# Free choice of PSUM banks, a new order table, and 114 VectorE instructions handed to GpSimd

## The chip, the cores and the metric

The kernel runs on one core of a Trainium2 chip. A core has five engines that work side by side and meet only at semaphores: TensorE (PE, the matmuls), ScalarE (ACT, the exponentials), VectorE (DVE), GpSimd (POOL) and SyncE (SP, which issues the DMAs). Operands lie in SBUF; matmul results land in PSUM, which has eight banks of 512 fp32 values for each of the 128 partitions. The metric is the device time of one execution in microseconds (us).

## The reference

Input x has 2048 rows of 640 values, in bfloat16. The output is `x + s * g`, with

```python
xn = _layernorm(x, axis=-1)
s = _A_ref(xn, A_wqkv, A_wo)                       # attention, 32 heads of 20
g = _silu(_B_ref(xn, B_w1, B_w2, B_w3, B_w4))
# A: qkv = xn @ wqkv; p = softmax(q k^T * 20**-0.5); s = (p v) @ wo
# B: h = gelu(layernorm(xn) @ w1); hs = [four quarters of h, shifted by 1, -1, 2, -2 rows] @ w2
#    x1 = xn + hs; result = x1 + gelu(layernorm(x1) @ w3) @ w4
```

So there are three layer norms: the one of x, the one inside `B` before w1, and the third one, of x1, before w3. The bulk of the work is the softmax: 32 heads times 2048 x 2048 exponentials.

## The kernel before

**Tasks and the order table.** The Python code does not issue instructions in the order in which it is written. Each piece of work is a task (`T(engine, cost, function, reads, writes, ...)`): a group of matmuls, one ACT, DVE or GpSimd instruction, or a DMA issue. After all 5483 tasks are known, `Planner.follow(TABLE)` reads a long string, `TABLE`: two characters name the next task, and one more character per acquisition says which banks (or which buffers) it takes. The string thus fixes the order of the instructions on every engine and the place of every PSUM tile. Each engine then works through its own list in that order, and a semaphore wait stands wherever a task needs another engine's result or a bank that another task has to give back. The costs, the `due` times and constants such as `c_pool`, `dma_bw` and `dma_lat0` only feed the planner that wrote the table; they issue nothing.

**Attention.** The heads are worked in eight quads of four heads, each quad in four groups of 512 queries (`attn_quad`): 32 groups. A group goes over 16 key tiles of 128 keys. For each key tile, PE makes scores (keys on the partitions, 512 queries, four heads: four banks), something turns scores into exp(scores), and PE multiplies these with the values into one bank, bank 7, which gathers the whole group (L1233 and L1367). A score tile (two heads, 1024 columns, two neighbouring banks) goes one of two ways:

- ACT takes the exponential straight out of PSUM (L1432, 788 instructions of 1024 columns; L1414 does two tiles in one instruction).
- Up to eight key tiles of a group are *block units*: two key tiles in a block, mostly two blocks in a unit. In a unit, ACT does half of each key tile. DVE does the other half with integer arithmetic: an eviction (L1459, tasks `u...`) writes 16-bit integers whose bit pattern is approximately exp as a bfloat16, and three more *bit pieces* per unit (L1358, tasks `s<quad>_<group>_<block>_<v>`, v = 1, 2, 3) add a constant to all 4096 integers (2048 in a unit of one block). Each of the four variants (the eviction's own and three pieces) is then multiplied with the values (L1367, tasks `pvd...`), and the four together average the error out.

**Two ways to make a score tile.** In row mode (L1375, `score`) the matmul takes the 32 partitions of one head, and the four heads use the four row groups of the array. In column mode (L1390) the queries lie in a zero-padded copy, and a tile takes eight matmuls of 128 rows and 32 columns. A task marked `flex` (496 single ACT tiles, `score_act`) takes row mode where the task before or behind it on PE is also in row mode, and column mode elsewhere; so the table decides that too.

**PSUM.** Banks 0 to 6 are handed out by `pl.kind(...)` in `build`: `S` (a score tile) may lie in banks 0-1 or 2-3; `W` (any projection or MLP tile, `mm_tile`, L640) in bank 4, 5 or 6; `SD` (the two score tiles of one block key: one for ACT, one for DVE) in one of the two pairs plus two of banks 4 to 6, or in both pairs. The transposes at the start use banks 0 to 3 in turn, and a task `gate` stands between them and the first score.

**End of a group.** `normalise`: DVE transposes bank 7 into SBUF (L1480), takes the reciprocal of the sums (L1482), multiplies (L1488, tasks `onT`, the reciprocal product), transposes back (L1490, tasks `on`), and SP stores the result to DRAM.

**Around it.** Everything else (projections of later heads, the whole of B, the output projection) is cut into `W` tiles that the table strews between the scores: PE makes a tile (L640), DVE evicts it (L1109, L1171, L1712, L1744, L1783, L1798, L1567 ...). The third norm is L872 on DVE, 16 of its 25 instructions, each 640 values out of and into SBUF. At the end, `finish_qc` adds x to each of 16 row tiles (L1628, tasks `cmb0` to `cmb15`, both inputs in SBUF) and stores them. The last group is worked in two halves (`last_half`) so that its output projection can begin early. GpSimd has memsets, small powers (L862), four early norms (L868, L910) and 17 scalings of values (L1179, L1512).

Of the kernel before, what the change touches and what calls it, by code (L numbers as in the profile page):

```python
# [57 lines left out]
class Planner:  # L58
    def __init__(self):
# [14 lines left out]
        self.dma_bw = 223.0  # L74
        self.dma_lat0 = 1900.0
# [141 lines left out]
    def follow(self, table):  # L217
# [24 lines left out]
        while at < len(table):  # L242
# [7 lines left out]
            st = max(row_at + 6.0, row_end[t.part]) if e == "pe" and pe_mode and t.mode else eng_free[e]  # L250
# [27 lines left out]
            if e == "pe":  # L278
                if t.mode != pe_mode:
                    t.finish += self.mode_cost  # L280
                if t.mode:
                    row_at = t.finish - t.dur
                    row_end[t.part] = t.finish
                pe_mode = t.mode
# [169 lines left out]
class Cfg:  # L454
# [5 lines left out]
    def __init__(self, S=2048, D=640, H=32, F=1536):  # L460
# [26 lines left out]
        self.AHEAD = 2  # L487
        self.UNITS = ((),
# [3 lines left out]
                      ((0, 0, 2), (1, 1, 2), (3, 0, 2), (5, 1, 2)))  # L492
# [25 lines left out]
            [4, 3, 2, 4])  # L518

# [44 lines left out]
def c_pe(ninstr, N):  # L564
    return ninstr * max(14.0, 0.106 * N)
# [5 lines left out]
def c_pool(n, kind="ts"):  # L571
    return 150 + (1.1 if kind == "ts" else 2.4) * n


class Gen:
# [8 lines left out]
    def alloc(self, name, shape, dtype):  # L584
# [4 lines left out]
        off = self.pl.alloc(name, n * esz)  # L589
# [26 lines left out]
    def T(self, eng, dur, fn, reads=(), writes=(), name="", **kw):  # L616
        kw.setdefault("cls", self.cur_cls)
        return self.pl.task(eng, dur, fn, reads=reads, writes=writes, name=name, **kw)
# [28 lines left out]
    def build(self, plan_only=False):  # L647
        nc, pl = self.nc, self.pl
        with contextlib.ExitStack() as es:
            ARENA = 212480  # L650
# [7 lines left out]
            pairs = [(0, [0, 1]), (0, [2, 3])]  # L658
            high = [(0, [4, 5]), (0, [5, 6]), (1, [4, 6])]
            third = [(1, x[1]) for x in high[:2]]  # L660
            pl.kind("W", "B", [(0, [4]), (0, [6]), (1, [5])])
            pl.kind("S", "B", pairs + (third if self.cfg.THIRD else []))
            pl.kind("SD", "B", [(r + q, x + y) for r, x in pairs for q, y in high]
                    + ([(3, pairs[0][1] + pairs[1][1]), (3, pairs[1][1] + pairs[0][1])] if self.cfg.FALL else []))
            pl.kind("SR", "B", [(r + q, x + y) for r, x in pairs for q, y in high[:2]]
                    + [(3, pairs[0][1] + pairs[1][1]), (3, pairs[1][1] + pairs[0][1])])
            pl.kind("SW", "B", [(0, [2, 3, 4, 5])])
            pl.hold = {"pe": self.cfg.HPE, "dve": self.cfg.HDVE}
            if self.cfg.SAVE:
                pl.saves = {"SD": "W", "SR": "W", "SW": "W"} if self.cfg.SAVE != 3 else {"SD": "W"}  # L670
                pl.reserve = self.cfg.RESERVE
                pl.hard = self.cfg.SAVE == 2
            pl.pool("PT", 7)
            pl.kind("PT", "PT", [(0 if i == 6 else 1, [i]) for i in range(7)])
            pl.kind("PT2", "PT", [(0, [i, i + 1]) for i in (0, 2, 4)])
# [13 lines left out]
    def program(self):  # L689
# [14 lines left out]
        self.T("pe", 0, None, writes=[("S", b) for b in range(4)] + [("gate",)], name="gate")  # L704
# [62 lines left out]
    def alloc_persistent(self):  # L767
# [37 lines left out]
        for b in range(4):  # L805
            self.pl.pe_psum_atoms.add(("S", b))
        self.pl.pe_psum_atoms.update([("PV", 0), ("wob",), ("ktp",), ("gate",)])
# [27 lines left out]
    def ln_tiles(self, tag, tiles, dst_of, dst_atoms_of, ve_out=None):  # L835
# [28 lines left out]
        for li, n in enumerate(tiles):  # L864
# [6 lines left out]
            T("dve", c_dve(D, "4x") + 140,  # L871
# [67 lines left out]
    def ln1_and_transpose(self):  # L939
# [13 lines left out]
        for g in range(4):  # L953
            for kc in range(cfg.KC):
                b = bk % 4
                act = bk in cfg.TRA
                bk += 1
                for bi in range(4):
                    n = 4 * g + bi
                    def fn(e, n=n, bi=bi, b=b, kc=kc):  # L960
                        pb = self.bank(b, BF16)
# [5 lines left out]
                    T("pe", c_pe(4, 128), fn, reads=[A("xn", n), A("ident")], writes=[("S", b)], name=f"tr_x{g}_{kc}_{n}")  # L967
                d = xnT[:, kc, 512 * g:512 * g + 512]
                if act:
                    T("act", c_act(512), lambda e, d=d, b=b: e.activation(d, self.bank(b, BF16)[:, 0:512], AF.Copy),  # L970
                      reads=[("S", b)], writes=[A("xnT", kc, g)], name=f"trev_x{g}_{kc}")
                else:
                    T("dve", c_dve(512, "2x"), lambda e, d=d, b=b: e.tensor_copy(d, self.bank(b, BF16)[:, 0:512]),
                      reads=[("S", b)], writes=[A("xnT", kc, g)], name=f"trev_x{g}_{kc}")
# [366 lines left out]
    def block_bits(self, quad, qc, blocks, ends):  # L1341
# [9 lines left out]
        for v in range(4):  # L1351
            if v == 0:
                dst, dsta = U[:, ub, 0:w], halves
            else:
# [3 lines left out]
                T("dve", c_dve(w, "4x"), lambda e, v=v, dst=dst: e.tensor_scalar(dst, U[:, ub, 0:w], EXP_B[v], None, op0=ALU.add),  # L1358
# [19 lines left out]
    def score_act(self, b, qc, kt, a, gb=None):  # L1378
# [4 lines left out]
        def fn(e):  # L1383
            for jj in range(2):
# [4 lines left out]
                for c in range(4):  # L1389
# [4 lines left out]
                    reads=[("gate",), A("KT", b, kt // 4), A("QT", b, qc), A("QTa", b, qc)] + ([] if gb is None else [A("QM", gb)]),  # L1394
# [3 lines left out]
    def score_rows(self, b, qc, kt, wide):  # L1398
# [7 lines left out]
        T("pe", 207, fn, reads=[("gate",), A("KT", b, kt // 4), A("QT", b, qc), A("QTa", b, qc)],  # L1406
# [31 lines left out]
    def score_both(self, b, qc, kt, a, quad, r):  # L1438
# [14 lines left out]
        T("pe", 207, fn, reads=[("gate",), A("KT", b, kt // 4), A("QT", b, qc), A("QTa", b, qc)], writes=[sa, da],  # L1453
# [12 lines left out]
    def normalise(self, quad, qc):  # L1466
# [22 lines left out]
        T("dve", c_dve(512, "1x"), fnn, reads=[A("Ob"), A("RZ", ob)], writes=[ota], name=f"onT{quad}_{qc}", cls=cls)  # L1489
# [115 lines left out]
    def finish_qc(self, qc):  # L1605
# [8 lines left out]
        for nl in range(4):  # L1614
# [13 lines left out]
            T("dve", c_dve(cfg.D, "2x"), lambda e, sl=sl, addend=addend, res=res: e.tensor_tensor(res, SB2[:, sl, :], addend, op=ALU.add),  # L1628
# [131 lines left out]
    def b_w34(self, c0):  # L1760
# [29 lines left out]
        for hh in range(2):  # L1790
# [3 lines left out]
            for n in range(4 * c0, 4 * c0 + 8):  # L1794
# [10 lines left out]
                T("dve", c_dve(2 * D, "1x"),  # L1805
# [7 lines left out]
    r"###^#6#q#_#f#(#3$)#]#}#)#$#7#[$9#8$D$Z#c$O&p#9#`#:#a#;#d#%#<#0#b&q#=&o$#$*#>#e#~#?(m#&#,$$#@(n#/$+#'#A#*$%#-#B$&$,#C#+#2$'#D#1#.#s$($-#E#F#u#G#H#v#I#4"  # L1813
# [119 lines left out]
```

## Time and profile before

| what | value |
|---|---|
| time, median of 3 runs (lowest to highest) | 863.0 us (862.06 to 863.29) |
| span of the profiled execution, first to last instruction | 859.6 us |
| busy: ACT / PE / DVE / POOL | 815.5 / 800.6 / 734.7 / 39.3 us |
| ACT exponentials of 1024 columns | 788 x 1039 ns |
| DVE evictions of a unit, 1024 columns | 189 x 1213 ns |
| DVE bit pieces of 4096 / 2048 | 150 x 1216 ns / 24 x 680 ns |
| mean granted TensorE clock | 0.988 of full speed |

The profiled execution is one by itself; the profile gives its span, and no other time of its own is shown. The median of the timed runs is 3.4 us above that span, which is taken as what lies before the first and behind the last instruction. An engine's busy time is the union of its instructions. A line such as "L1432 ACT ACTIVATE arena<-psum 128x1024 bf16<-128x1024 f32 x788" names the source line, the engine, the operation, output and input with their shapes, and the number of instructions. The name `arena` is the one SBUF tensor that holds everything. In the views of waits, the engine that stood still is on the left, and what released it is behind the arrow. Durations of neighbouring instructions of one engine overlap a little, since one begins while the one before it still drains.

### The profile page before, as it was taken

How to read it: one execution, taken by the hardware profiler on the slowest of the kernel's cores; microseconds unless marked ns; L12 is line 12 of the kernel's file. 1: busy time of each engine (PE TensorE's matmuls, PEld its weight loads, DVE VectorE, ACT ScalarE, POOL GpSimd, SP SyncE). 2: the span in 40 equal slices, each digit the busy share in tenths (PEclk: the TensorE clock that was granted, in tenths of full speed). 3: DMA queues.
4: the chain of work that ended last, by engine and by line, in shares of the span. 5: the costliest groups of instructions: out<-in, count | busy, mean ns of one | idle time of the engine just before them, and what ended most of it. 6: DMA issues, size and time to landing. Idle time of an engine off the chain costs nothing.

```text
span 859.6 us, 31925 instructions
## 1 busy us (share of the span) xinstructions
PE 800.6 (93%) x14542; PEld 338.8 (39%) x14542; DVE 734.7 (85%) x1031; ACT 815.5 (95%) x854; POOL 39.3 (5%) x75
## 2 busy tenths in 40 slices
PE   7999999999899999999988999999997899989996
PEld 4443333334344433333433444343333343424464
DVE  7649999998998899999877999998995889987655
ACT  7799999999999999999999999999999999999994
POOL 5510000000000000000000000000000000000000
PEclk9999999999999999999999999999999999999998
DMA  7000533222110022311033011313211102041312
GB/s 230 18 16 24 137 97 89 90 66 65 25 40 16 18 50 55 79 44 46 11 94 92 14 51 27 81 36 89 50 32 47 34 13 54 13 123 33 116 57 95
DMA packets 74487, 50.83 MB, mean 59 GB/s; under 512 B 44768, under 2 KB 69552, under 8 KB 74352
## 3 DMA queue, kind: packets, MB, share of 16 engines
q1 hardware_dynamic: 74352, 48.79, 21.1%
q8 instruction: 115, 1.88, 0.9%
q14 instruction: 20, 0.16, 0.1%
HBM read 34.53 MB, written 10.17 MB: 52 GB/s over the span
## 4 chain that ended last, share of the span: by engine, by line
ACT 63%; PE 29%; DVE 7%; issue 1%; DMA 1%; SPq 0%; DVEq 0%
ACT arena L1432 57%; PE psum L640 10%; PE psum L1375 5%; PE psum L1390 4%; PE psum L1367 3%; PE psum L1233 3%; DVE arena L1459 2%; ACT arena L1787 2%; PE psum L1274 1%; ACT arena L1803 1%; DVE arena L1358 1%; ACT arena L1414 1%; ACT arena L1716 1%; DVE arena L852 1%; PE psum L963 1%
## 5 line engine op out<-in xcount | busy, mean ns | idle before, releaser
L1432 ACT ACTIVATE arena<-psum 128x1024 bf16<-128x1024 f32 x788 | 733.1, 1039 | 20.8 <-PE psum L1375 17.8
L640 PE MATMUL psum<-arena 128*32 128x320 bf16 (+1 forms) x5952 | 359.2, 335 | 0.6 <-DVE arena L1459 0.2
L1459 DVE TENSOR_SCALAR arena<-psum 128x1024 uint16<-128x1024 f32 (+1 forms) x243 | 263.7, 1094 | 31.8 <-PE psum L1375 30.5
L640 PEld LDWEIGHTS psum<-arena 128*32 128x32 bf16 x5952 | 148.8, 97 | 132.6 <-issue 31.2
L1375 PE MATMUL psum<-arena 32*128 32x512 bf16 x1384 | 165.6, 387 | 34.6 <-ACT arena L1432 24.2
L1358 DVE TENSOR_SCALAR arena<-arena 128x4096 uint16<-128x4096 uint16 (+1 forms) x174 | 194.7, 1142 | 2.9 <-PE psum L1367 1.8
L1390 PE MATMUL psum<-arena 128*32 128x512 bf16 x2400 | 182.7, 381 | 3.1 <-ACT arena L1432 2.1
L1233 PE MATMUL psum<-arena 128*22 128x512 bf16 x1552 | 148.9, 383 | 2.4 <-ACT arena L1432 2.0
L1367 PE MATMUL psum<-arena 128*22 128x512 bf16 x1728 | 146.2, 381 | 3.3 <-DVE arena L1358 3.1
L1375 PEld LDWEIGHTS psum<-arena 32*128 32x128 bf16 x1384 | 42.0, 91 | 179.5 <-ACT arena L1432 115.1
L1390 PEld LDWEIGHTS psum<-arena 128*32 128x32 bf16 x2400 | 46.1, 95 | 69.3 <-ACT arena L1432 57.7
L1367 PEld LDWEIGHTS psum<-arena 128*22 128x22 bf16 x1728 | 40.6, 91 | 53.6 <-issue 15.5
L1233 PEld LDWEIGHTS psum<-arena 128*22 128x22 bf16 x1552 | 38.8, 91 | 49.9 <-issue 18.6
L1109 DVE CAST arena<-psum 128x512 bf16<-128x512 f32 x40 | 27.0, 682 | 11.7 <-PE psum L640 11.4
L1783 DVE CAST arena<-psum 128x512 bf16<-128x512 f32 x48 | 32.7, 681 | 3.0 <-PE psum L640 2.5
L1567 DVE SCALAR_TENSOR_TENSOR arena<-psum,arena 128x320 bf16<-128x320 f32 x32 | 15.5, 489 | 22.5 <-PE psum L640 22.3
L1171 DVE CAST arena<-psum 128x320 bf16<-128x320 f32 x32 | 15.1, 486 | 16.2 <-PE psum L640 16.0
L852 DVE BATCH_NORM_STATS2 arena<-arena 128x6 f32<-128x320 bf16 x54 | 23.7, 477 | 3.2 <-DMA arena<-in_A_x_dram 3.1
L1480 DVE STREAM_TRANSPOSE arena<-psum 128x512 f32<-128x512 f32 x31 | 21.9, 708 | 1.7 <-PE psum L1367 1.2
L1490 DVE STREAM_TRANSPOSE arena<-arena 128x512 bf16<-128x512 bf16 x31 | 21.8, 702 | 0.2
L1744 DVE TENSOR_TENSOR arena<-psum,arena 128x320 bf16<-128x320 f32 x32 | 15.1, 480 | 7.2 <-PE psum L640 7.0
L1488 DVE TENSOR_TENSOR arena<-arena 128x512 bf16<-128x512 f32 x31 | 21.1, 680 | 0.1
(118 smaller groups left out, 364.2 us busy)
## 6 DMA issues: line engine op xcount, KB each, us to landing
arena<-in_B_w_dram SPq DMA_DIRECT2D x48, 160.0 KB, 2.6
arena<-arena SPq DMA_DIRECT2D x124, 32.0 KB, 2.2
arena<-in_B_w_dram SPq DMA_DIRECT2D x4, 960.0 KB, 5.7
arena<-in_A_x_dram SPq DMA_DIRECT2D x8, 320.0 KB, 5.9
arena<-in_A_x_dram SPq DMA_DIRECT2D x16, 160.0 KB, 2.3
out_dram<-arena SPq DMA_DIRECT2D x16, 160.0 KB, 1.8
heads<-arena SPq DMA_DIRECT2D x112, 20.0 KB
arena<-keys SPq DMA_DIRECT2D x28, 80.0 KB
```

The source lines that it names most:

```text
L640: ins = e.matmul(pb[32 * c:32 * c + 32, 0:N], lhsT(k, c), rhs(k, c), start=(k == 0), stop=(stop and k == nk - 1), tile_position=(0, 32 * c))
L852: lambda e, li=li, n=n, hh=hh: e.bn_stats(st[:, li, 6 * hh:6 * hh + 6], xn[:, n, hD * hh:hD * hh + hD]),
L1109: T("dve", c_dve(512), lambda e, h=h, c=c: e.tensor_copy(KS[:, 512 * c:512 * c + 512], self.wbank(h)[:, 0:512]), reads=[wa], writes=[A("KS ...
L1233: ins = e.matmul(pb[32 * i:32 * i + 22, 0:512], VA[:, ql, kts[i // 2], i, :], PT[:, slots[i // 2][0].slot, 512 * (i % 2):512 * (i % 2) + 512],
L1358: T("dve", c_dve(w, "4x"), lambda e, v=v, dst=dst: e.tensor_scalar(dst, U[:, ub, 0:w], EXP_B[v], None, op0=ALU.add), reads=halves, writes= ...
L1367: ins = e.matmul(pb[32 * i:32 * i + 22, 0:512], wv, dst[:, at:at + 512].bitcast(BF16), start=first, stop=final, tile_position=(0, 32 * i))
L1375: return e.matmul(out, self.KT[32 * i:32 * i + 32, b, 128 * kt:128 * kt + 128], self.QT[32 * i:32 * i + 32, b, 512 * qc:512 * qc + 512], s ...
L1390: ins = e.matmul(out[32 * c:32 * c + 32, :], self.KT[:, b, 128 * kt + 32 * c:128 * kt + 32 * c + 32], self.QM[:, gb, 2 * a + jj, :], start ...
L1432: lambda e: e.activation(self.PT[:, hp.slot, :], self.psum[:, 512 * hs.slot:512 * hs.slot + 1024], AF.Exp, scale=cfg.scale),
L1459: ins = e.tensor_scalar(U[:, ub, 1024 * at + 512 * k:1024 * at + 512 * k + w], self.psum[:, 512 * hd.slots[k]:512 * hd.slots[k] + w], a_ex ...
L1480: T("dve", c_dve(512), lambda e: e.transpose(Ob[:, :], self.bank(self.PVB)[:, :]), writes=[("PV", 0), A("Ob")], name=f"ob{quad}_{qc}", cls ...
L1783: T("dve", c_dve(512), lambda e, h=h, fc=fc, i=i: e.tensor_copy(GT[:, i, fc, :], self.wbank(h)[:, 0:512]), reads=[wa], writes=at, name=f"g ...
```

## The change

The change has six parts.

1. **Banks.** `W` may take any single bank of 0 to 6, `S` any two neighbouring banks, `SD`, `SR` and `SW` nearly any set of such pairs. The 20 transpose tiles at the start become `W` tiles, and the task `gate` goes.
2. **Bit pieces.** The piece v = 3 of every unit that begins at block 0 or 2 goes from DVE to GpSimd: 58 of the 174, of which 50 have 4096 columns and 8 have 2048. The instruction is the same `tensor_scalar` add of a constant, out of SBUF and into SBUF.
3. **Reciprocal products.** The product of L1488 goes to GpSimd in 28 of the 31 whole groups (all quads but the last).
4. **Third norm and last adds.** All 16 instructions of the third norm, and `cmb0` to `cmb11` of the 16 last adds, go to GpSimd. So GpSimd has 185 tasks instead of 71, and DVE has 890 instead of 1004.
5. **Planner constants and memory.** `dma_bw`, `dma_lat0`, `c_pool` and the model of row mode are other numbers; the arena is 352 bytes larger and the third norm's small tiles are packed closer.
6. **The table.** `TABLE` is new throughout. ACT has the same 837 tasks and PE the same ones but `gate`, in another order. Read against the rule for `flex`, the new order puts 285 of the 496 flexible score tiles in row mode and 211 in column mode (196 and 300 before), and PE goes from one mode to the other 712 times (610 before). The number of evictions that are split in two instructions, because their two banks do not touch, goes from 27 to 31.

```diff
@@ -71,8 +71,8 @@
-        self.dma_bw = 223.0
-        self.dma_lat0 = 1900.0
+        self.dma_bw = 260.0
+        self.dma_lat0 = 1800.0
...
@@ -516,6 +529,11 @@
+        self.PN = True
+        self.P3 = tuple(range(16))
+        self.PC = tuple(range(12))
+        self.PP = {(quad, qc, 0, 3) for quad in range(8) for qc in range(4)} | {(quad, qc, 2, 3) for quad in range(8) for qc in range(4)}
...
@@ -569,7 +587,7 @@
 def c_pool(n, kind="ts"):
-    return 150 + (1.1 if kind == "ts" else 2.4) * n
+    return 90 + (1.25 if kind == "ts" else 2.2) * n
...
@@ -655,24 +673,16 @@
-            pairs = [(0, [0, 1]), (0, [2, 3])]
-            high = [(0, [4, 5]), (0, [5, 6]), (1, [4, 6])]
-            third = [(1, x[1]) for x in high[:2]]
-            pl.kind("W", "B", [(0, [4]), (0, [6]), (1, [5])])
-            pl.kind("S", "B", pairs + (third if self.cfg.THIRD else []))
-            pl.kind("SD", "B", [(r + q, x + y) for r, x in pairs for q, y in high]
-                    + ([(3, pairs[0][1] + pairs[1][1]), (3, pairs[1][1] + pairs[0][1])] if self.cfg.FALL else []))
-            pl.kind("SR", "B", [(r + q, x + y) for r, x in pairs for q, y in high[:2]]
-                    + [(3, pairs[0][1] + pairs[1][1]), (3, pairs[1][1] + pairs[0][1])])
...
+            pairs = [[i, i + 1] for i in (0, 2, 1, 3, 4, 5)]
+            pl.kind("W", "B", [(0, [4]), (0, [6]), (1, [5])] + [(3, [i]) for i in range(4)])
+            pl.kind("S", "B", [(2 * (k > 1), p) for k, p in enumerate(pairs)])
+            pl.kind("SD", "B", [(2 * (k > 1) + 2 * (y > x + 1), p + [x, y]) for k, p in enumerate(pairs) for x in range(6, -1, -1)
+                                for y in range(x + 1, 7) if x not in p and y not in p])
+            pl.kind("SR", "B", [(2 * (k > 1), p + q) for k, p in enumerate(pairs) for q in pairs if not set(p) & set(q)])
+            pl.kind("SW", "B", [(0, [2, 3, 4, 5]), (0, [0, 1, 2, 3]), (1, [1, 2, 3, 4]), (1, [3, 4, 5, 6])])
             pl.pool("PT", 7)
             pl.kind("PT", "PT", [(0 if i == 6 else 1, [i]) for i in range(7)])
+            pl.kind("PT2", "PT", [(i % 2, [i, i + 1]) for i in (0, 2, 4, 1, 3, 5)])
...
@@ -701,7 +711,6 @@
         self.b_stages = self.b_branch()
-        self.T("pe", 0, None, writes=[("S", b) for b in range(4)] + [("gate",)], name="gate")
         for quad in range(cfg.NQUAD):
...
@@ -868,7 +875,8 @@
-            T("dve", c_dve(D, "4x") + 140,
+            onp = not ve_out and n in cfg.P3
+            T("pool" if onp else "dve", c_pool(D) if onp else c_dve(D, "4x") + 140,
               lambda e, li=li, n=n: e.tensor_scalar(dst_of(n), xn[:, n, :], mv[:, li, 0:1], rs[:, li:li + 1],
                                                     op0=ALU.subtract, op1=ALU.mult),
               reads=[A("xn", n), A(tag + "_mv", li), A(tag + "_rs")], writes=dst_atoms_of(n), name=f"{tag}_norm{n}", lock=True)
...
@@ -952,26 +960,27 @@
-                b = bk % 4
+                h, wa = self.wtile()
...
-                    T("pe", c_pe(4, 128), fn, reads=[A("xn", n), A("ident")], writes=[("S", b)], name=f"tr_x{g}_{kc}_{n}")
+                    T("pe", c_pe(4, 128), fn, reads=[A("xn", n), A("ident")], writes=[wa], name=f"tr_x{g}_{kc}_{n}",
+                      acq=("W", h) if bi == 0 else None, tile=h.id)
...
@@ -1355,7 +1364,9 @@
                 dst, dsta = SS[:, k, 0:w], [A("SS", k)]
-                T("dve", c_dve(w, "4x"), lambda e, v=v, dst=dst: e.tensor_scalar(dst, U[:, ub, 0:w], EXP_B[v], None, op0=ALU.add),
+                onp = (quad, qc, blocks[0][0], v) in cfg.PP
+                T("pool" if onp else "dve", c_pool(w) if onp else c_dve(w, "4x"),
+                  lambda e, v=v, dst=dst: e.tensor_scalar(dst, U[:, ub, 0:w], EXP_B[v], None, op0=ALU.add),
                   reads=halves, writes=dsta, name=f"s{quad}_{qc}_{blocks[0][0]}_{v}", lock=True, due=self.at(self.nact, f"s{quad}"))
...
@@ -1486,7 +1497,9 @@
-        T("dve", c_dve(512, "1x"), fnn, reads=[A("Ob"), A("RZ", ob)], writes=[ota], name=f"onT{quad}_{qc}", cls=cls)
+        onp = cfg.PN and not last
+        T("pool" if onp else "dve", c_pool(512, "tt") if onp else c_dve(512, "1x"), fnn, reads=[A("Ob"), A("RZ", ob)], writes=[ota],
+          name=f"onT{quad}_{qc}", cls=cls, lock=True)
         T("dve", c_dve(512, "1x"), lambda e: e.transpose(dst, OnT), reads=[ota], writes=dsta, name=f"on{quad}_{qc}", cls=cls)
...
@@ -1625,7 +1638,8 @@
-            T("dve", c_dve(cfg.D, "2x"), lambda e, sl=sl, addend=addend, res=res: e.tensor_tensor(res, SB2[:, sl, :], addend, op=ALU.add),
+            onp = n in cfg.PC
+            T("pool" if onp else "dve", c_pool(cfg.D, "tt") if onp else c_dve(cfg.D, "2x"), lambda e, sl=sl, addend=addend, res=res: e.tensor_tensor(res, SB2[:, sl, :], addend, op=ALU.add),
               reads=adda + [A("SB2", sl, 0), A("SB2", sl, 1)], writes=resa, name=f"cmb{n}", lock=True, cls=-2 if split and nl > 1 else 0)
             T("sp", C_SP, lambda e, res=res, n=n: e.dma_start(outv[:, n, :], res),
...
 TABLE = (
-    r"###^#6#q#_#f#(#3$)#]#}#)#$#7#[$9#8$D$Z#c$O&p#9#`#:#a#;#d#%#<#0#b&q#=&o$#$*#>#e#~#?(m#&#,$$#@(n#/$+#'#A#*$%#-#B$&$,#C#+#2$'#D#1#.#s$($-#E#F#u#G#H#v#I#4"
...
+    r"#3###6#(#,&p&q#^#$#q#7$##/#0#~#f$*#8#9#]#_#[#:#;#<$+$,#=$-#>#?$.#@$9#)#c#%$$$%#u#s#`$[#v#r#A#B#d#C#&#'#*#}$&#D#E#F$'#t#w#x#G#H$)$(%9(#y#h#g#I#j#J#K#-#"
...
```

## The prediction, made before the changed kernel was run

> **What bounds the kernel now.** I read the page first: busy time and the chain that ended last.
>
> ```profile
> span 859.6 us, 31925 instructions
> PE 800.6 (93%) x14542; PEld 338.8 (39%) x14542; DVE 734.7 (85%) x1031; ACT 815.5 (95%) x854; POOL 39.3 (5%) x75
> ...
> ACT 63%; PE 29%; DVE 7%; issue 1%; DMA 1%; SPq 0%; DVEq 0%
> ```
>
> ACT is the bound, and its work isn't touched. Next I cut the span at the first exponential (33.66) and the end of the last (848.57). Columns: stretch and length, then busy us of PE, PEld, DVE, ACT and POOL.
>
> ```profile
> 0.00:33.66 33.66, 28.02 (x676) 15.74 (x680) 24.69 (x89) 21.52 (x40) 15.77 (x44) 0.95 0.52 154
> 33.66:848.57 814.91, 769.47 (x13803) 321.25 (x13803) 702.64 (x928) 793.96 (x814) 23.50 (x32) 0.99 0.21 55
> 848.57:859.60 11.03, 3.13 (x78) 1.86 (x66) 7.39 (x15) 0.00 (x1) 0.00 (x0) 0.71 0.25 91
> ```
>
> In the middle ACT idles 814.91 - 793.96 = 21.0 us, in the head 12.1, in the tail 11.0. So even a perfect order saves 21 us in the middle and a few at the ends. The waits of ACT say for whom it idles:
>
> ```profile
> ACT arena L1432 <- PE psum L1375: 17.8, 35, 0.9
> ACT arena L970 <- PE psum L963: 4.5, 4, 2.4
> ```
>
> The exponentials wait for scores, never longer than 0.9 us: PE comes late, in small steps. The chain by line shows what stands on the path:
>
> ```profile
> by line: ACT arena L1432 56.6%; PE psum L640 10.5%; PE psum L1375 4.9%; PE psum L1390 4.2%; PE psum L1367 3.1%; PE psum L1233 2.9%; DVE arena L1459 2.5%; ACT arena L1787 2.4%; PE psum L1274 1.3%; ACT arena L1803 1.1%; DVE arena L1358 1.1%;
> ```
>
> The groups by shape give prices (us busy, mean ns | idle before, by releaser):
>
> ```profile
> L1358 DVE TENSOR_SCALAR arena<-arena 128x4096 uint16<-128x4096 uint16 x150 | 179.0, 1216 | 0.9
> L1390 PE MATMUL psum<-arena 128*32 128x512 bf16 x2400 | 182.7, 381 | 3.1 <-ACT arena L1432 2.1 <-ACT arena L1414 0.6
> L1375 PE MATMUL psum<-arena 32*128 32x512 bf16 x1384 | 165.6, 387 | 34.6 <-ACT arena L1432 24.2 <-DVE arena L1459 8.3 <-DVE arena L1075 0.5
> ```
>
> Last, the timeline of GpSimd beside DVE (start, us), and GpSimd's groups, for prices and for what they do to each other:
>
> ```profile
> 35.30 2.90 POOL L1664 TENSOR_TENSOR arena<-arena 128x16 f32<-128x16 f32 x1
> 41.63 1.27 POOL L1164 MEMSET arena<- 128x256 bf16 x1
> ...
> 37.53 0.28 DVE L1009 TENSOR_SCALAR arena<-arena 128x512 uint16<-128x512 uint16 x1
> 41.97 1.07 DVE L1009 TENSOR_SCALAR arena<-arena 128x512 uint16<-128x512 uint16 x1
> ```
>
> ```profile
> L1179 POOL TENSOR_SCALAR arena<-arena 128x176 bf16<-128x176 bf16 x16 | 5.9, 379 | 240.5 <-DVE arena L1171 240.5
> L868 POOL TENSOR_SCALAR arena<-arena 128x640 bf16<-128x640 bf16 x2 | 1.8, 880 | 0.6 <-DVE arena L898 0.4
> ```
>
> The same DVE instruction takes 0.28 us alone and 1.07 us when it begins inside a GpSimd memset, which it outlasts (42.90 against 43.04): it waited for the memset's end. Inside L1664, a slow power of 16 elements, it took 0.28: no wait.
>
> **The change, part by part.**
>
> *PE (order table).* A column-mode tile costs 182.7/300 = 0.609 us of PE, a row-mode one 2 x 165.6/1384 = 0.239. Now 89 tiles change to row mode: 33 us less PE work. On the chain stands 4.2% of 859.6 = 36.1 us of L1390; of that 89/300 x (1 - 0.239/0.609) goes: **-6.5 us**. Against it, 51 more entries into row mode. No row shows such an entry alone; PE's idle before L1375 (34.6 us over 305 entries) caps it at 0.11 us, 5.8 us on PE, of which the chain sees PE's 29%: 0 to 1.7, I take **+1**, the middle.
>
> *DVE relief.* Off DVE go 50 pieces of 1.19 us (179.0/150), 8 of 0.65, 28 products of 0.68, 16 norms of 0.41 and 12 adds of 0.48: 96 us of 735. Only what stands on the chain counts: L1358 has 1.1%, 9.5 us, and a third of it (58/174) goes: **-3.2 us**. Products, norms and adds show no share worth a line; zero.
>
> *GpSimd's own time.* 640 elements take 0.88 us, 176 take 0.34 when nothing disturbs them: 1.16 ns an element, so a 4096 piece takes 4.9 us as an estimate. Ends: 3.5 us (slope between the 176 row and L1512's 352 elements in 0.484) and 5.6 (slope from there to 640). I take the slope over the whole known span. 50 x 4.9 + 8 x 2.5 = 265 us. Two-input work has no row: between the one-input price and twice it, 0.73 to 1.5 us a product and 0.88 to 1.8 an add. All in all some 330 us of 860, so GpSimd itself isn't the bound. Does it come late? In PE's new order the product with piece 3 stands 7 to 21 score tiles behind its unit's last score (mean 13.6; before, 3 to 23, mean 9.5). Seven tiles are 7.3 us of ACT; score, eviction and piece need 0.24 + 1.2 + 4.9 = 6.3. Covered, **0**; with the cover gone, PE stands at that product with all later scores behind it, and ACT loses what exceeds about two tiles in PSUM, 2.1 us. The reciprocal products queue behind a piece in 25 of 28 cases; DVE's transpose back stands 1.6 to 26.7 us of DVE work behind the reciprocal (0.6 to 19.5 before), so it's the two or three shortest that may wait, and the store behind it isn't needed until the last quad: 0. The stores of tiles 0 to 11 wait for GpSimd instead of DVE, and SP's later loads queue behind them; the third norms feed transposes that the table places later. No DMA is added: 0, some tenths at worst.
>
> *The shared port.* Here DVE pays. I walked the new table: behind each piece on GpSimd, I summed the DVE evictions and transposes that stand before DVE's next instruction of the kind that waited at 41.97 (bit pieces; I take adds and products with two SBUF inputs along). 15 of 58 pieces are covered by that work; 12 have at most one eviction. The shortfall is 110 us for pieces at 4.9 us, and 18 us for the rest. If DVE waits as at 41.97 and has nothing else to wait for, it is occupied 735 - 96 + 128 = 767 us instead of 735; if as at 37.53, 639. What does that do to ACT? Over 25 us stretches from 75 to 825, the 16 with DVE at 23 us or more (mean 24.0) have 0.71 us of ACT idle, the other 14 (mean 20.1) 0.54: 0.043 us of ACT per us of DVE. 128 x 0.043 = 5.5. Ends: 0 and the lumps below; I take **+5.5**, since the memset row is nearer to a streaming piece than the power is.
>
> The Trainium skill, page "SBUF — State Buffer", section "Who interferes with whom", makes this a rule: GpSimd and a DVE instruction in a two-port mode (or with two SBUF inputs, against a GpSimd read) hold the shared port pair by an exclusive lock for a whole instruction, and the loser blocks fully. The memset row agrees (1.07 against 0.28 us), the power row doesn't (0.28). By the rule the forecast is as here, and lumps are its bad case; without any wait it would be 5.5 us lower, 852.
>
> *Banks.* Transposes may use seven banks. ACT's waits for them are 4.5 us, 2.4 of it the first, which no bank shortens: 0 to 2.1, I take **-1**. Four more split evictions cost DVE 4 x 0.15: nothing.
>
> *Tail.* Before, two evictions L1586 and two adds L1628 (0.72, 0.49, 0.74, 0.49) stand on the chain between the transpose of the last half at 850.21 and its product. In the new DVE order three come ahead of that transpose and one behind the transpose back, where DVE waits 0.83 us for PE anyway. 0 to 2.4; half, **-1.2**.
>
> Sum: -6.5 + 1 - 3.2 + 5.5 - 1 - 1.2 = -5.4. On the span 859.6 that is 854.2; with the 3.4 us between span and median (863.0), **857.6**.
>
> **The rivals.**
>
> *Lumps at the port: slower.* In the 12 units with no more than one eviction, a 4.9 us wait comes in one piece. Evictions queue behind it, PE stops at a tile whose bank isn't given back, and ACT lives on two tiles: 4.9 - 2.1 = 2.8 us lost each. It decides from two lumps on (5.6 against 5.4). Half of the 12: 857.6 + 16.8 = 874; all: 891. For it: nothing orders the two engines at the port, so a delay of tenths turns a wait of 1.2 us by GpSimd into one of 4.9 by DVE. Against: the DVE in question would often wait for scores at that time (46 waits of L1459, 30.5 us).
>
> *Late pieces: slower.* At 2.5 ns an element a piece takes 10.4 us, with eviction and score 11.8, and the nine shortest covers (7, 7, 9, 9, 10, 10, 11, 11, 11 tiles) lack 18 us together: 876. Against: twice the known slope.
>
> *The order does more.* If PE's 33 us and DVE's slack halve the 21 us of idle in the middle, with the ends: 863 - 10.5 - 2.2 = 850; the floor is 840.
>
> *Nothing.* The relieved work was beside the path, and another chain through PE (L640, 10.5%) is as long: 863.
>
> **How the numbers follow.** Forecast, a few us less: 0.42 (852 to 861). More: 0.12 (850). Within 0.2%, about what a measurement of this kernel can tell from no change: 0.09. Lumps: 0.27 (874). Late pieces and what I don't see in a wholly new order: 0.10 (876 and up). Faster 0.54, same 0.09, slower 0.37. The range 846 to 881 leaves out the best of "more" and lumps from about nine on, some 0.17.
>
> **What would show it.** Right: 211 column tiles (1688 matmuls at L1390), DVE near 640 us plus waits, pieces on POOL at 3.5 to 5.6 us, ACT idle in the middle below 21 us. Port: bit pieces left on DVE with durations far above 1.2 us. Late: PE waiting at L1367 for POOL. Wrong if ACT's idle in the middle rises, with DVE or PE standing for over 2 us in front of it.

## The result and the profile after

The changed kernel takes 1274.4 us (median; 1273.2 to 1275.8), the kernel before 862.8 beside it: a ratio of 1.477, interval 1.475 to 1.479. It is 48% slower, where 857.6 us was forecast and 881 was the top of the range. The profiled execution took 1273.2 us, its span is 1271.5.

The page of the changed kernel: busy time, shares of the chain that ended last by engine, and the costliest groups (line, engine, shapes, count | busy us, mean ns of one | idle before it, and the releaser of most of it).

```profile
span 1271.5 us, 30914 instructions
PE 885.0 (70%) x14008; PEld 343.9 (27%) x14008; DVE 971.8 (76%) x921; ACT 828.9 (65%) x854; POOL 735.7 (58%) x189
...
DVE 31%; PE 30%; POOL 22%; ACT 10%; issue 8%; DMA 0%; SPq 0%; POOLq 0%; DVEq 0%
...
L1443 ACT ACTIVATE arena<-psum 128x1024 bf16<-128x1024 f32 x788 | 746.4, 1036 | 426.9 <-PE psum L1386 302.6
L1369 POOL TENSOR_SCALAR arena<-arena 128x4096 uint16<-128x4096 uint16 (+1 forms) x58 | 598.4, 10317 | 354.8 <-PE psum L1378 192.7
L1369 DVE TENSOR_SCALAR arena<-arena 128x4096 uint16<-128x4096 uint16 (+1 forms) x116 | 413.2, 3576 | 5.6 <-PE psum L1378 4.2
```

The same group of ACT in the kernel before:

```profile
L1432 ACT ACTIVATE arena<-psum 128x1024 bf16<-128x1024 f32 x788 | 733.1, 1039 | 20.8 <-PE psum L1375 17.8
```

ACT's instructions are the same, but it idles 426.9 us in front of its exponentials where it idled 20.8: 406 of the 412 us that the span grew. Two prices are new. A bit piece on GpSimd takes 10.3 us in the mean, more than twice the forecast. And the pieces that *stayed* on DVE take 3576 ns in the mean where the two forms took 1216 and 680: 116 of them cost 413 us instead of some 130. Other short DVE work grew too, an instruction of six elements (L1074) from 0.21 to 2.30 us. DVE, relieved of 96 us of work, is busy 972 us instead of 735; a stopped instruction counts as busy.

The timeline of the changed kernel (start, us; in brackets what the engine had been idle for) shows one such collision:

```profile
107.21 1.23 DVE L1369 TENSOR_SCALAR arena<-arena 128x4096 uint16<-128x4096 uint16 x1
107.26 11.57 POOL L1369 TENSOR_SCALAR arena<-arena 128x4096 uint16<-128x4096 uint16 x1 [6.85 <-DVE arena L1470]
...
108.35 1.22 DVE L1470 TENSOR_SCALAR arena<-psum 128x1024 uint16<-128x1024 f32 x1
...
110.08 9.83 DVE L1369 TENSOR_SCALAR arena<-arena 128x4096 uint16<-128x4096 uint16 x1
...
119.97 0.61 PE L1378 MATMUL psum<-arena 128*22 128x512 bf16 x4 [6.75 <-DVE arena L1369]
...
122.44 1.02 ACT L1443 ACTIVATE arena<-psum 128x1024 bf16<-128x1024 f32 x1 [7.84 <-PE psum L1386]
```

The piece on GpSimd waits about 1 us for DVE's piece and ends at 118.83. DVE's eviction out of PSUM takes its 1.22 us inside it. DVE's next piece starts at 110.08, stands until GpSimd ends, and is done 1.08 us later, at 119.91. PE stands 6.75 us for that piece with the scores behind it, and ACT stands 7.84 us for the scores. In the whole trace 38 of DVE's 100 pieces of 4096 begin inside a GpSimd piece and take 8.61 us in the mean, and 37 of these end 1.08 us behind it; the other 62 take 1.24 us. The waits say the same in sums (us, times, longest):

```profile
PE psum L1378 <- DVE arena L1369: 125.3, 20, 10.6
PE psum L1378 <- POOL arena L1369: 65.7, 20, 5.6
```

So both suspects of the prediction are at work: pieces that come late from GpSimd (65.7 us of PE), and DVE stopped at the port (125.3 us of PE behind its pieces alone). The experiments take them apart.

### The profile page after: what moved, and what is told of

It is laid out like the page before. It is cut to its first block, busy times and chain, and to the rows that moved or that the text cites. A ratio compares the mean times of both kernels' runs of the same rounds, so it can differ in the third digit from the quotient of the medians.

```text
span 1271.5 us, 30914 instructions
## 1 busy us (share of the span) xinstructions
PE 885.0 (70%) x14008; PEld 343.9 (27%) x14008; DVE 971.8 (76%) x921; ACT 828.9 (65%) x854; POOL 735.7 (58%) x189
## 3 DMA queue, kind: packets, MB, share of 16 engines
HBM read 34.53 MB, written 10.17 MB: 35 GB/s over the span
## 4 chain that ended last, share of the span: by engine, by line
DVE 31%; PE 30%; POOL 22%; ACT 10%; issue 8%; DMA 0%; SPq 0%; POOLq 0%; DVEq 0%
DVE arena L1369 20%; POOL arena L1369 19%; PE psum L658 11%; ACT arena L1443 9%; PE psum L1386 5%; PE psum L1378 5%; DVE arena L1470 4%; PE psum L1401 4%; PE psum L1242 3%; POOL arena L880 2%; DVE arena L1491 1%; DVE arena L1499 1%; DVE arena L1074 1%; DVE arena L1118 1%; DVE arena L1797 0%
## 5 line engine op out<-in xcount | busy, mean ns | idle before, releaser
L1443 ACT ACTIVATE arena<-psum 128x1024 bf16<-128x1024 f32 x788 | 746.4, 1036 | 426.9 <-PE psum L1386 302.6
L1369 POOL TENSOR_SCALAR arena<-arena 128x4096 uint16<-128x4096 uint16 (+1 forms) x58 | 598.4, 10317 | 354.8 <-PE psum L1378 192.7
L1369 DVE TENSOR_SCALAR arena<-arena 128x4096 uint16<-128x4096 uint16 (+1 forms) x116 | 413.2, 3576 | 5.6 <-PE psum L1378 4.2
L658 PE MATMUL psum<-arena 128*32 128x320 bf16 (+1 forms) x5952 | 384.7, 362 | 37.2 <-DVE arena L1726 9.9
L1378 PE MATMUL psum<-arena 128*22 128x512 bf16 x1728 | 172.9, 431 | 192.8 <-DVE arena L1369 125.3
L1386 PE MATMUL psum<-arena 32*128 32x512 bf16 x1562 | 198.2, 428 | 124.2 <-DVE arena L1470 41.0
L1242 PE MATMUL psum<-arena 128*22 128x512 bf16 x1552 | 164.9, 426 | 1.3 <-DVE arena L1491 0.8
L1401 PE MATMUL psum<-arena 128*32 128x512 bf16 x1688 | 146.8, 428 | 10.3 <-DVE arena L1797 9.4
L1386 PEld LDWEIGHTS psum<-arena 32*128 32x128 bf16 x1562 | 47.8, 93 | 307.3 <-issue 109.1
L1499 POOL TENSOR_TENSOR arena<-arena 128x512 bf16<-128x512 f32 x28 | 36.2, 1291 | 63.7 <-DVE arena L1493 43.9
L1401 PEld LDWEIGHTS psum<-arena 128*32 128x32 bf16 x1688 | 40.9, 106 | 65.2 <-ACT arena L1443 25.7
L880 POOL TENSOR_SCALAR arena<-arena 128x640 bf16<-128x640 bf16 x16 | 42.4, 2656 | 0.3
L1642 POOL TENSOR_TENSOR arena<-arena 128x640 bf16<-128x640 bf16 x12 | 17.9, 1494 | 36.7 <-DVE arena L1580 31.1
```

The source lines that it names most:

```text
L658: ins = e.matmul(pb[32 * c:32 * c + 32, 0:N], lhsT(k, c), rhs(k, c), start=(k == 0), stop=(stop and k == nk - 1), tile_position=(0, 32 * c))
L880: lambda e, li=li, n=n: e.tensor_scalar(dst_of(n), xn[:, n, :], mv[:, li, 0:1], rs[:, li:li + 1], op0=ALU.subtract, op1=ALU.mult),
L1242: ins = e.matmul(pb[32 * i:32 * i + 22, 0:512], VA[:, ql, kts[i // 2], i, :], PT[:, slots[i // 2][0].slot, 512 * (i % 2):512 * (i % 2) + 512],
L1378: ins = e.matmul(pb[32 * i:32 * i + 22, 0:512], wv, dst[:, at:at + 512].bitcast(BF16), start=first, stop=final, tile_position=(0, 32 * i))
L1386: return e.matmul(out, self.KT[32 * i:32 * i + 32, b, 128 * kt:128 * kt + 128], self.QT[32 * i:32 * i + 32, b, 512 * qc:512 * qc + 512], s ...
L1401: ins = e.matmul(out[32 * c:32 * c + 32, :], self.KT[:, b, 128 * kt + 32 * c:128 * kt + 32 * c + 32], self.QM[:, gb, 2 * a + jj, :], start ...
```

## The experiments

"Time" is the median, with the ratio to the kernel before, run beside it.

**Prices alone.** A small program, GpSimd alone first, then one DVE instruction inside a GpSimd piece.

> Nothing of the reference is computed: the output is zeros, and GpSimd runs single instructions by themselves, then one bit piece each time while VectorE tries one instruction inside it. In the changed kernel an undisturbed piece of 4096 takes 10.54 us, one of 2048 5.36. Theory 'form': GpSimd is slow at a lone add and quick at multiply-and-add, whatever the type, since the rows that gave 1.16 ns an element were all multiply-and-add: add 10.5 us on both uint16 and bfloat16, multiply-and-add near 4.9 us on both; subtract-then-multiply of 640 near 2.5 us, multiply-and-add of 640 near 0.88. Theory 'type': the 16-bit integers are slow: 10.5 us for both forms on uint16, near 4.9 for both on bfloat16. Theory 'port': GpSimd is slow only beside VectorE: all forms near 4.9 us when alone. For VectorE inside a piece: if a port is held for a whole GpSimd instruction, the piece of VectorE (1.2 us alone), the add of two SBUF operands and the tiny tensor_scalar wait some 9 us, to the end of the piece, and the eviction out of PSUM, the transpose and the statistics don't wait.

Its timeline:

```profile
17.11 10.54 POOL L35 TENSOR_SCALAR pool_out<-pool_in 128x4096 uint16<-128x4096 uint16 x1 [2.49 <-DVE ps L87]
...
33.18 3.60 POOL L37 TENSOR_SCALAR pool_out<-pool_in 128x4096 uint16<-128x4096 uint16 x1
...
38.84 10.54 POOL L39 TENSOR_SCALAR pool_outb<-pool_inb 128x4096 bf16<-128x4096 bf16 x1
49.46 3.60 POOL L40 TENSOR_SCALAR pool_outb<-pool_inb 128x4096 bf16<-128x4096 bf16 x1
53.17 0.87 POOL L41 TENSOR_SCALAR pool_outb<-pool_inb,scal 128x640 bf16<-128x640 bf16 x1
54.15 2.51 POOL L42 TENSOR_SCALAR pool_outb<-pool_inb,scal 128x640 bf16<-128x640 bf16 x1
...
97.84 10.56 POOL L65 TENSOR_SCALAR pool_out<-pool_in 128x4096 uint16<-128x4096 uint16 x1
...
99.31 10.17 DVE L92 TENSOR_SCALAR dve_out<-dve_in 128x4096 uint16<-128x4096 uint16 x1
...
119.74 1.23 DVE L94 TENSOR_SCALAR dve_out<-ps 128x1024 uint16<-128x1024 f32 x1
...
142.49 7.68 DVE L98 TENSOR_TENSOR dve_outb<-dve_inb 128x640 bf16<-128x640 bf16 x1
...
153.49 9.10 DVE L100 TENSOR_SCALAR dve_outb<-dve_f 128x6 bf16<-128x6 f32 x1
```

L35 and L39 are a lone add, L37 and L40 multiply-by-1-and-add on the same data: 10.54 against 3.60 us, for uint16 as for bf16. So it is the form, not the type, and nothing on DVE is needed for it. L41 is multiply-and-add with per-row scalars, the form of the 640-element row that the prediction took its price from; L42 is subtract-then-multiply, the third norm: 2.51 against 0.87. And a DVE piece that begins inside a lone add ends 1.08 us behind it (10.17 us instead of 1.23), an instruction of six elements with it (9.10 instead of 0.23); an eviction out of PSUM isn't held up (1.23). An add of two SBUF inputs took 7.68 instead of 0.49, but was through at 150.17, before the lone add around it (141.02 to 151.56) had ended; transposes and norm statistics were undisturbed.

**Undoing parts of the change.** Pieces back on DVE, then all work back (only banks, constants and the new table stay):

```diff
-        self.PP = {(quad, qc, 0, 3) ...} | {(quad, qc, 2, 3) ...}
+        self.PP = ()
```

```diff
-        self.PN = True
-        self.P3 = tuple(range(16))
-        self.PC = tuple(range(12))
-        self.PP = {(quad, qc, 0, 3) ...} | {(quad, qc, 2, 3) ...}
+        self.PN = False
+        self.P3 = ()
+        self.PC = ()
+        self.PP = ()
```

> The changed kernel with its 58 bit pieces back on VectorE, all else as changed (new table, banks, products, norms and adds on GpSimd). Theory 'price of the piece': nearly all of the loss goes; VectorE has 704 us of work and few long waits, 850 to 880 us. Rival 'the new order or the banks': they lose by themselves, still above 1100 us.

> The changed kernel with all 114 instructions back on VectorE: only the new table, the banks and the constants stay. Theory 'price of the piece': 845 to 870 us, so the order with 89 more row-mode tiles is worth between +2% and -1%. Rival 'the new order or the banks': above 1100 us.

879.8 us (1.022; 1.019 to 1.024) and 893.3 (1.035; 1.032 to 1.038). The pieces make 395 of the 412 us. The first is at the top of what was expected. The second was a miss: the new order without its offload is not a little faster than the old one, it is 3.5% slower. Its groups show where two thirds of that are (idle time before, by releaser, at the end; the same group of the kernel before stands below it):

```profile
L1378 PE MATMUL psum<-arena 128*22 128x512 bf16 x1728 | 153.1, 385 | 23.8 <-DVE arena L1369 23.8
...
L1367 PE MATMUL psum<-arena 128*22 128x512 bf16 x1728 | 146.2, 381 | 3.3 <-DVE arena L1358 3.1
```

PE stands 23.8 us at the products for a piece of DVE, against 3.1 us before. Presumably the order places them as if GpSimd had made one piece in three.

**The quick form.** The piece on GpSimd as multiply by 1 and add:

```diff
-e.tensor_scalar(dst, U[:, ub, 0:w], EXP_B[v], None, op0=ALU.add)
+e.tensor_scalar(dst, U[:, ub, 0:w], 1.0, EXP_B[v], op0=ALU.mult, op1=ALU.add)   # on GpSimd only
```

> The changed kernel with the 58 pieces on GpSimd as multiply by 1.0 and add (the same values). Theory 'form': a piece takes near 4.9 us and the kernel comes to 850 to 890 us. Theory 'type': pieces stay at 10.5 us and the kernel at 1274.

922.2 us (1.071; 1.068 to 1.075): 352 us better by the form alone, but above what was expected. DVE is still busy 730 us, its 4096 pieces still take 1896 ns in the mean.

**The old order.** The same two moves of the pieces in the kernel before:

> The kernel before, its own order table, banks and constants, with one edit: the pieces of 96 (piece 3) of the units that begin at block 0 or 2 are made on GpSimd, with the lone add. Theory (the piece's 10.5 us and the port, whatever the order): the product with piece 3 stands closer behind its unit here (3 to 23 tiles, mean 9.5, against 7 to 21), so it loses at least what the new order loses to the same move (1274 - 880 = 394 us): 1200 to 1350. Rival (the new order is what suffers, an order with other neighbours would not): below 1000.

> As the run with the old order and the lone add, but the piece is multiply by 1 and add 96, 3.6 us instead of 10.5. Theory: 3.6 us is 2.4 later than on DVE, at the closest places one to two tiles late, and a DVE instruction caught at the port loses up to 2.4: 58 pieces lose 0 to 2 us each, 863 to 960, middle 900. Rival (the move is good once the piece is quick, the new table is what costs): 850 to 863.

1438.5 us (1.668) and 1020.7 (1.182; 1.178 to 1.186), both above the expectation. So it isn't the new order that suffers: the old one ends 164 and 99 us above the new one with the same pieces. (The other moves are left out here; a later run puts them at 12 us.)

**Port or lateness?** Two runs, each with one of the two. In the first nobody waits for the piece:

```diff
+                if onp:
+                    dst = None            # the product reads a part of VA instead
...
-                  reads=dsta + ...
+                  reads=([A(f"VA{hf}", k) for k in range(6)] if dst is None else dsta) + ...
```

> The changed kernel, pieces on GpSimd with the lone add as they are, but TensorE's product with such a piece reads a part of the values instead of the piece (so the output is not the reference's): nothing waits for the piece, and the port is as busy as in the changed kernel. If the port alone makes the loss: 1230 to 1280. If the wait for the late piece alone makes it: 860 to 900. If both, in series: in between, 1000 to 1200.

1319.7 us (1.530; 1.527 to 1.534), above even the range for the port alone. Nobody waits for GpSimd's pieces, and it is even slower than the changed kernel:

```profile
PE 887.3 (67%) x14008; PEld 345.9 (26%) x14008; DVE 1080.5 (82%) x921; ACT 827.9 (63%) x854; POOL 754.0 (57%) x189
...
DVE 44%; PE 33%; ACT 13%; issue 7%; POOL 1%; DMA 1%; SPq 0%; DVEq 0%
...
L1369 DVE TENSOR_SCALAR arena<-arena 128x4096 uint16<-128x4096 uint16 (+1 forms) x116 | 532.4, 4605 | 5.5 <-PE psum L1381 4.4
```

GpSimd has 1% of the chain, DVE 44%. The port alone is enough for the whole loss. (With the waits DVE is stopped less, 972 us busy against 1080, and 38 of its pieces of 4096 take over 1.6 us against 50: where PE waits for GpSimd, DVE waits with it, for scores. That reading is argued from these numbers.)

In the second, the piece is late and the port short:

```diff
+        e.tensor_tensor(self.still[:, 0:k], one, one, op=ALU.pow)     # k = 40, or 20 for a short piece
+        return e.tensor_scalar(dst, src, 1.0, add, op0=ALU.mult, op1=ALU.add)
```

> The changed kernel with the quick piece (3.6 us), and ahead of each piece on GpSimd a power of 40 fp32 elements on scratch of its own (20 for a short piece), about 7 us by the 2.90 us of 16 elements, during which DVE took its normal time in the trace of before: the piece comes as late as with the lone add, but holds the port for 3.6 us only. If lateness makes the loss: 1200 to 1280. If the port makes it: 920 to 1000 (the quick piece alone gave 922). If the power holds the port after all, DVE's durations during it say so, and the run tells nothing.

1008.7 us (1.170; 1.166 to 1.174), a little above the range for the port and far below the one for lateness. The power took 7386 ns, and the 39 DVE pieces of 4096 that lie wholly inside one took 1.22 us in the mean, so it leaves the port free. Against 922.2 with the same piece and no delay, lateness costs 86 us, or somewhat more, since DVE's pieces of 4096 stood less at the port here (1434 ns in the mean against 1896). It comes from PE at the product (L1386 in this kernel):

```profile
PE psum L1386 <- POOL arena L1356: 103.1, 41, 5.4
```

**Shorter holds.** A hold is the time for which one GpSimd instruction keeps the port from DVE. If it is one instruction long, the same work in several instructions should free DVE. Lone adds of 512 elements, and multiply-adds of 1024, with and without the norms:

```diff
+[e.tensor_scalar(dst[:, x:x + c], U[:, ub, x:x + c], EXP_B[v], None, op0=ALU.add) for x in range(0, w, c)]   # c = 512
```

```diff
+[e.tensor_scalar(dst[:, x:x + 1024], U[:, ub, x:x + 1024], 1.0, EXP_B[v], op0=ALU.mult, op1=ALU.add) for x in range(0, w, 1024)]
```

> The changed kernel, each GpSimd piece made by lone adds of 512 elements, eight for a whole piece (1.4 us each by the slope of 10.54 and 5.36 us), so it comes as late as before or later (11.5 us), but no instruction is longer than 1.4 us. If the port is held for one instruction and then given to the other engine: DVE loses about 1.4 us an instruction instead of up to 10.5, and the time is near that of the late piece with a free port: 950 to 1060. If GpSimd keeps the port while its instructions stand back to back: above 1230.

> The changed kernel, each GpSimd piece made by multiply-by-1-and-add of 1024 elements, four for a whole piece (about 1.05 us each), no wait of DVE longer than that. If the whole quick piece (922) still loses by the length of its hold: 880 to 905. If it loses for other reasons (norms, the new order): 915 to 930.

> As the run with four quick instructions to a piece, and the 16 third norms back on DVE (0.41 us there; 2.66 us of GpSimd and of the port each, in the changed kernel). If the norms cost about their hold at the port: 10 to 30 us below that run, at best even with the kernel before (855 to 890). If they lie beside other work: within 5 us of it.

Eight lone adds: 1123.0 us (1.303), between the two ranges. Four multiply-adds: **848.5 us** (0.985; 0.982 to 0.988), below both ranges. With the norms back: 850.8 (0.986; 0.984 to 0.988), no difference, though each norm takes GpSimd 2.7 us. The lone adds are the lateness in its pure form:

```profile
PE 872.8 (78%) x14008; PEld 339.8 (30%) x14008; DVE 676.6 (60%) x921; ACT 826.8 (74%) x854; POOL 840.1 (75%) x563
...
POOL 61%; PE 20%; ACT 10%; DVE 5%; issue 3%; DMA 1%; SPq 0%; POOLq 0%; DVEq 0%
...
L1369 POOL TENSOR_SCALAR arena<-arena 128x512 uint16<-128x512 uint16 x432 | 712.7, 1678 | 187.0 <-DVE arena L1470 106.0 <-PE psum L1378 80.9
...
PE psum L1378 <- POOL arena L1369: 187.9, 47, 6.6
```

DVE is as free as with four multiply-adds (676.6 us against 676.0), so the port is no longer the matter, and GpSimd has become the chain: 61% of it.

The page and the groups by shape of the kernel with four multiply-adds:

```profile
PE 785.7 (93%) x14008; PEld 325.6 (38%) x14008; DVE 676.0 (80%) x921; ACT 814.0 (96%) x854; POOL 406.7 (48%) x347
...
ACT 55%; PE 25%; DVE 15%; POOL 2%; DMA 2%; issue 1%; SPq 1%; DVEq 0%
...
L1443 ACT ACTIVATE arena<-psum 128x1024 bf16<-128x1024 f32 x788 | 732.2, 1048 | 16.8 <-PE psum L1386 7.4
...
L1369 DVE TENSOR_SCALAR arena<-arena 128x4096 uint16<-128x4096 uint16 x100 | 139.9, 1412 | 3.7 <-PE psum L1378 2.5
```

ACT idles 16.8 us before its exponentials (20.8 before the change) and has 55% of the chain again.

**Threshold or proportion, and whose gain it is.** Two and eight instructions to a piece; the old order with four; the new order with the pieces alone:

```diff
-range(0, w, 1024)    # 1024 elements each
+range(0, w, 2048)    # and, in another run, 512
```

> The changed kernel, each whole GpSimd piece made by two multiply-by-1-and-adds of 2048 elements (1.90 us each). It lies between one instruction of 3.60 us (922) and four of about 1.05 (848). The lumps of the prediction (a wait of DVE costs ACT what exceeds the 2.1 us of two tiles in PSUM): 1.9 is below 2.1, so nothing is lost, 846 to 856; the same sum gives 848 + 50 x (3.6 - 2.1) = 923 for one instruction, measured 922. Rival, loss in proportion to the hold: (922 - 848)/(3.6 - 1.05) = 29 us per us, 848 + 0.85 x 29 = 873, so 866 to 880.

> The changed kernel, each whole GpSimd piece made by eight multiply-by-1-and-adds of 512 elements (about 0.63 us each by the slope of 3.60 and 1.90). The time fell from 867.5 to 848.5 when the hold went from 1.90 to 1.05 us, 22 us per us. If that goes on: 848 - 0.42 x 22 = 839, so 836 to 844. Rival: at four the waits are down to what does no harm, and a piece of more instructions comes later: 846 to 856.

867.5 us (1.006; 1.004 to 1.008) and **845.7 us** (0.980; 0.977 to 0.982). A threshold at a hold of 2.1 us is out: holds of 1.9 us cost 19 us more than holds of 1.05. Below that the curve flattens; the last run fell between its two expectations.

| piece on GpSimd, new order | one hold, us | DVE busy, us | time, us |
|---|---|---|---|
| lone add, nobody waits | 10.54 | 1080.5 | 1319.7 |
| lone add (the changed kernel) | 10.54 | 971.8 | 1274.4 |
| one multiply-add | 3.60 | 730.0 | 922.2 |
| two | 1.90 | 692.6 | 867.5 |
| four | 1.05 | 676.0 | 848.5 |
| eight | 0.61 | 668.5 | 845.7 |

The work of DVE is the same in all rows; what differs is how long it stood at the port. From four to two, a microsecond more on DVE costs 19.0/16.6 = 1.15 us, from two to one 54.7/37.4 = 1.46, and from eight to the run in which nobody waits 474/412 = 1.15; from eight to four it is 2.8/7.5 = 0.37, no more than the runs of one kernel scatter. What lies above 1 may in part be TensorE's own: its score matmuls of L1401 take 384 ns in the mean with four multiply-adds, at a granted clock of 0.99, and 428 ns in the changed kernel at 0.84. No run takes the two apart.

> The kernel before, its own order, with only the pieces of 96 moved to GpSimd, four quick instructions each: short holds, but a piece that takes some 5 us instead of 1.2 and stands 3 to 23 tiles ahead of its product. If the new order is needed for the move to gain (its products stand 7 to 21 tiles behind): 870 to 950. If the move gains in any order, and the new table adds nothing: 845 to 862.

> The changed kernel with four quick instructions to a piece, and norms, products and last adds back on DVE (31 us of work). DVE was busy 676 of 846 us with them moved, so it has room: 848 to 856, as with all of them moved. Rival: these moves carry what is gained over the kernel before, 858 to 870.

943.9 us (1.094; 1.092 to 1.096) and 860.4 (0.998; 0.997 to 0.999): the first as expected if the new order is needed, the second in the range of the rival. In the old order even the quick piece in four comes late for its product:

```profile
PE psum L1368 <- POOL arena L1359: 42.5, 24, 4.6
```

And in the new order the pieces alone just reach the time of before; the other moves, 31 us of DVE work, bring 12 us more. By the run with the norms back (850.8), most of these 12 are the products and the last adds.

## Why the prediction was wrong, step by step

*What bounds it.* Right: ACT stands for PE in small steps, and what stops PE or DVE comes out in ACT's idle time. What this meant for a wait of several microseconds wasn't drawn from it. (The 3.4 us added from span to median mix two executions: where a run's time and span are both on record, they differ by 1.7 to 3.2 us.)

*GpSimd's own time: the first step that failed.* 1.16 ns an element was read from rows that all multiply and add; the lone add costs 10.54 us/4096 = 2.57 ns. The ends, 3.5 and 5.6 us, missed it by half: they bounded the slope, and not the form. (For the multiply-and-add, 3.60 us, the lower end was right.) The third norm failed the same way (0.88 us expected, 2.66 in the changed kernel), though it is harmless. The two-input work lay within its bounds (1.29 us a product, 1.49 an add). "GpSimd itself isn't the bound" fell with it: at this price it is busy 736 us, and in eight lone adds it has 61% of the chain.

*The shared port: the step that made the error large.* The mechanism was right: what waits is a bit piece or a two-input instruction, evictions and transposes don't. (Instructions of a few elements wait too, which it left out.) Of the two factors, the wait was sized at 128 us; between the changed kernel and the one with the shortest holds it is 971.8 - 668.5 = 303, and 271 of it are DVE's pieces (413.2 us against 142.0). Most of the excess goes with the long piece: at a hold of 3.60 us it is 730.0 - 668.5 = 62. The other factor, 0.043 us of ACT per us of DVE, was off by 27 or more: it is 1.15 to 1.46 for all but the shortest holds. With 1.15, even the 128 us would have been 147 us, and the forecast about 1000. It was read from stretches in which DVE was a little busier, and busy time has slack; a stopped DVE has none. The evictions queue behind the stopped instruction, PE issues in order, and ACT has two tiles in hand. The Trainium skill, page "SBUF — State Buffer", section "Who interferes with whom", says that the loser blocks fully for a whole instruction; the traces agree for the pieces (10.17 us for a piece of 1.23 inside a lone add of 10.56), but not for the add of two SBUF inputs, which got through 1.39 us before the end. Dividing the instruction divides the wait.

*The rivals.* "Lumps at the port" was the right mechanism with both sizes wrong. A lump was priced at what exceeds the 2.1 us of two tiles; two multiply-adds show that no such allowance applies to each hold (1.9 us holds, 19 us lost). And 12 units were thought to be exposed, since evictions cover the others; in the changed kernel 37 of the 58 pieces caught a piece of DVE. "Late pieces" named 10.4 us a piece, almost the measured 10.54, but by luck: no row stood behind the 2.5 ns. And it priced it at 18 us by the nine shortest covers. Lateness alone costs 86 us (power and multiply-add, 11.0 us a piece) or 277 (eight lone adds, 13.4 us, against eight multiply-adds). The covers were counted as if a piece started right behind its unit's eviction; in the run with eight lone adds GpSimd sits idle before 52 of the 58 pieces, 29 times until an eviction is done and 23 times until a product on PE is, presumably the one that reads the buffer which the piece fills. How much of the 277 us that makes wasn't tried. "Twice the known slope", the argument against the rival, had one form behind it.

*Order table.* The count was right, 1688 matmuls in column mode, but the 33 us less PE work were 15 (785.7 us busy in four multiply-adds, 800.6 before), though the two groups of score matmuls fell by 35 together (348.3 to 312.9): presumably a part of a group's time runs beside other matmuls, so that a tile's share of it is more than the tile costs. And the term can't stand by itself. The new order loses 31 us with DVE making every piece, and gains 13 with quick, short-held pieces and the other moves on GpSimd; the old order loses 82 with the quick pieces in four. So no run shows the -6.5 us by themselves.

*DVE relief.* -3.2 us was far too little for this order: all work back gives 893, pieces in four on GpSimd 860, norms, products and adds too 848. A chain share of 1% in the old order didn't say what the relief is worth in an order that counts on it.

*Banks and tail.* In the kernel with eight multiply-adds the first exponential starts at 29.4 us (33.7 before) and the span ends 7.4 us after the last (11.0 before). Together 8 us, where -2.2 was forecast; how much of it is banks and how much order wasn't tried.

## What to carry to other kernels

Before work goes to GpSimd, price the exact instruction there, operation by operation: a multiply by 1 in front of a lone add made the same piece three times faster. Then ask how long one instruction holds the port it shares with VectorE, and cut it into short ones: four or eight multiply-adds turned a change that lost 48% into one that gains 1.5 to 2%. A microsecond for which an in-order engine is stopped isn't a microsecond of its busy time; here it cost 1.15 to 1.46 us, and not the slope of its load, 0.043.

## What the runs showed of the hardware

- GpSimd `tensor_scalar`, 128 partitions: lone add 2.57 ns an element, multiply-and-add 0.88, in uint16 and bf16; with per-row scalars, 640 elements, 0.87 us multiply-add and 2.51 subtract-multiply.
- A DVE `tensor_scalar` of six elements waits for the port like one of 4096: 9.10 us instead of 0.23.
- Between back-to-back GpSimd instructions DVE gets in: among eight lone adds of 1.49 us its 4096 pieces took 1327 ns in the mean. A GpSimd power on fp32 doesn't stop them: 39 pieces inside one took 1.22 us in the mean.
- The granted TensorE clock was lower in the kernels in which PE stood more: 0.99 before, 0.84 in the changed kernel between 33.66 and 1260.00 us, 0.99 again with four multiply-adds.
